# A gated linear recurrence and a top-1 expert layer: chunk scores by one product per head, rows sorted by expert as they come, fixed places per expert

## The chip, the core and the metric

The kernel runs on one core of a Trainium2 chip. A core has TensorE (PE in the profile; its weight loads stand apart as PEld), VectorE (DVE), ScalarE (ACT), GpSimd (POOL) and SyncE (SP), each with an instruction queue of its own that it works off in order, and DMA engines that move data between HBM and the on-chip memories. The metric is the device time of one execution in microseconds. All data are fp32.

## What is computed

Two parts. The first is a recurrence with a decay per key dimension, over 768 tokens, for 4 batches of 8 heads with 48 dimensions; the second sends each of the 3072 tokens (all heads side by side, 384 values) to the one of 8 experts with the largest cosine to its embedding.

```
f = 1.0 / (1.0 + np.exp(-f_logit))
for t in range(S):
    state = f[:, :, t, :, None] * state + np.einsum('bhd,bhe->bhde', k[:, :, t], v[:, :, t])
    y[:, :, t] = np.einsum('bhd,bhde->bhe', q[:, :, t], state)
...
logits = xn @ en.T / tau
expert_idx = np.argmax(logits, axis=1)
...
for e in range(E):
    mask = expert_idx == e
    h = np.maximum(x[mask] @ w1[e], 0.0)          # w1[e]: 384 x 1024
    out[mask] = gate_w[mask, None] * (h @ w2[e])  # w2[e]: 1024 x 384
```

## The kernel before

Attention works in chunks of 128 tokens. `attend` takes a group of two chunks of one batch with all 8 heads, and two batches run half a group apart, so that one's products fill the other's waits. f, k and q are loaded as they lie (tokens on the partitions) and turned by transposes on PE (`turn`). Inside a chunk the score of a pair s < t needs the product of f from s+1 to t. The kernel builds it in seven levels m = 1 to 64 (L199 to L229): at each level PE multiplies all of kp by half the columns of qp (L203, 8 products a level and group), DVE puts the pairs that belong to this level into the score tile `am` under a mask (L210), DVE and POOL multiply qp and kp by the decays of the next level (L220, L223, L225). So a level's products wait for the step before them. Then the state's increment (kp turned, L240, times v, L246), the output y from the state (L265, 48 rows) and the scores (L268, 128 rows) in turn, the row x stored to `x_rows` in HBM (L290), its squared length (L294) and its logits (L297 to L305).

Routing starts when all 24 chunks are through: the gate, each token's rank within its expert, and a product with one-hot matrices (L422 to L434) that turns positions into a list of source rows for 31 blocks of 128 places.

The experts: for each of 31 blocks, `hidden` reads the block's expert number into registers, loads w2 (w1 of all experts was loaded during attention), gathers 128 rows (L460), turns them (L470) and multiplies them by w1 (L477, the rows stationary, 512 columns moving); `result` turns h (L492), multiplies it by w2 (L498) and scatters the rows to `out` (L507). Block j+1's `hidden` is issued ahead of block j's `result`.

The order on each engine is that of the program, as far as the scheduler of the tile layer leaves it; a tile's buffers are handed on in turn, and the one who wants one back waits for its last reader.

## Time and profile before

| | us |
|---|---|
| three timed runs | 1111.2, 1114.74 (median), 1120.58 |
| the profiled execution, first to last instruction | 1119.0 |
| attention | 9.4 to 630 |
| routing | 630 to 678 |
| experts | 678 to 1119 |

The rows are those of the profiled execution; times in it are microseconds from its first instruction. A group of rows names the line, the engine, the operation, what is written and read with shapes, and what the engine waited for ahead of it. [...]

### The profile page before, as it was taken

Reading aid. Unit: us, or ns where it says so; the run is one execution under the profiler, and the core shown is the slowest. Engines: PE = TensorE matmul, PEld = TensorE weight load, DVE = VectorE, ACT = ScalarE, POOL = GpSimd, SP = SyncE. Lnnn points to the kernel's source line nnn. Section 1 sums busy time; section 2 is a strip of 40 time slices with the busy share of each in tenths; the row PEclk is TensorE's granted clock in tenths of the full one; section 3 lists DMA queues with packets and bytes.
Section 4 is the critical chain, followed back from the end, with each engine's and each line's share of the span. In section 5 each row is a group of like instructions: output and inputs, shape, how many; then the busy total and the mean of one; then the engine's idle time right before and its main releaser. Section 6 shows DMA issues by size and latency. Waiting matters only on the chain. (4 is left out here: it accounts for less than half of the span.)

```text
span 1119.0 us, 10918 instructions
## 1 busy us (share of the span) xinstructions
PE 901.7 (81%) x4218; PEld 675.3 (60%) x4218; DVE 417.8 (37%) x523; ACT 125.2 (11%) x236; POOL 287.2 (26%) x315
## 2 busy tenths in 40 slices
PE   4687889888797978879897647888888888888886
PEld 3576878777686877768776543444444444444443
DVE  7558464563727385463723341111111111111111
ACT  3001101010101101010100100111111111111110
POOL 6325424151505245151511011111111111111101
PEclk8788787776858687775865558999999999999999
DMA  9907303030303123010100005444444444444430
GB/s 221 258 23 218 64 8 71 1 71 1 71 1 71 40 32 71 1 29 1 29 15 1 15 16 189 141 141 140 141 141 141 135 141 136 139 141 141 141 115 0
DMA packets 140802, 96.47 MB, mean 86 GB/s; under 512 B 102120, under 2 KB 134095, under 8 KB 140752
## 3 DMA queue, kind: packets, MB, share of 16 engines
q1 hardware_dynamic: 135280, 80.22, 27.3%
q0 software_dynamic: 5312, 15.54, 3.7%
q8 instruction: 34, 0.56, 0.2%
q14 instruction: 16, 0.13, 0.0%
q10 hardware_dynamic: 160, 0.01, 0.0%
HBM read 86.32 MB, written 10.81 MB: 87 GB/s over the span
## 5 line engine op out<-in xcount | busy, mean ns | idle before, releaser
L203 PE MATMUL sc<-qz,kp 128*128 128x128 f32 x1344 | 235.7, 347 | 82.1 <-DVE qz L220 68.0
L203 PEld LDWEIGHTS sc<-qz,kp 128*128 128x128 f32 x1344 | 222.0, 256 | 91.6 <-POOL kp L223 42.9
L498 PE MATMUL y_ps<-w_sb,hT 128*128 128x384 f32 x496 | 167.2, 491 | 39.5 <-issue 38.2
L477 PE MATMUL h_ps<-w_sb,xT 128*128 x372 | 169.6, 606 | 18.8 <-DVE xT L472 18.8
L210 DVE COPY_PREDICATED a<-mask,sc 128x1024 f32<-128x1024 uint8 x84 | 135.6, 1614 | 111.7 <-PE sc L203 110.6
L498 PEld LDWEIGHTS y_ps<-w_sb,hT 128*128 128x128 f32 x496 | 91.8, 190 | 103.5 <-issue 44.0
L223 POOL TENSOR_TENSOR kp<-kp,dec 128x512 f32<-128x512 f32 x72 | 85.6, 1189 | 180.8 <-PE sc L203 172.0
L477 PEld LDWEIGHTS h_ps<-w_sb,xT 128*128 128x128 f32 x372 | 69.0, 192 | 101.9 <-issue 75.8
L220 DVE TENSOR_TENSOR qz<-qz,dec 64x512 f32<-64x512 f32 x144 | 120.0, 833 | 2.2
L460 POOL DMA_INDIRECT xin<-x_rows,src_row x31 | 31.6, 1020 | 332.5 <-PE x_ps L470 315.9
L494 DVE COPY hT<-ht_ps 128x1024 f32<-128x1024 f32 x31 | 38.0, 1224 | 198.1 <-PE ht_ps L492 198.1
L268 PE MATMUL y<-v_ld,a 128*128 128x48 f32 x384 | 105.0, 379 | 0.0
L265 PE MATMUL y<-state,qz 48*128 48x48 f32 x320 | 96.8, 397 | 0.0
L268 PEld LDWEIGHTS y<-v_ld,a 128*128 128x128 f32 x384 | 80.4, 268 | 13.3
L472 DVE COPY xT<-x_ps 128x384 f32<-128x384 f32 x31 | 17.3, 558 | 179.5 <-PE x_ps L470 179.4
L265 PEld LDWEIGHTS y<-state,qz 48*128 48x128 f32 x320 | 72.3, 280 | 13.8 <-issue 0.9
L286 DVE TENSOR_TENSOR av<-y,av 128x768 f32<-128x768 f32 x12 | 11.5, 958 | 131.3 <-PE y L268 131.3
L485 ACT ACTIVATE h<-h_ps 128x1024 f32<-128x1024 f32 x31 | 31.8, 1025 | 218.2 <-PE h_ps L477 218.2
L507 POOL DMA_INDIRECT out_dram<-y,dst_row x31 | 31.3, 1011 | 63.2 <-ACT y L506 55.3
L506 ACT ACTIVATE y<-y_ps,gpos 128x384 f32<-128x384 f32 x31 | 18.0, 581 | 202.8 <-PE y_ps L498 195.9
L294 ACT ACTIVATE sq<-av 128x384 f32<-128x384 f32 x24 | 12.4, 516 | 242.6 <-DVE av L286 242.6
L492 PEld LDWEIGHTS ht_ps<-ident,h 128*128 128x128 f32 x248 | 29.0, 141 | 16.3 <-issue 15.8
(133 smaller groups left out, 616.8 us busy)
## 6 DMA issues: line engine op xcount, KB each, us to landing
w_sb<-in_moe_w_dram SPq DMA_DIRECT2D x39, 1536.0 KB, 7.9
f_ld<-in_f_logit_dram SPq DMA_DIRECT2D x24, 192.0 KB, 4.4
k_ld<-in_k_dram SPq DMA_DIRECT2D x24, 192.0 KB, 3.9
q_ld<-in_q_dram SPq DMA_DIRECT2D x24, 192.0 KB, 4.5
v_ld<-in_v_dram SPq DMA_DIRECT2D x24, 192.0 KB, 3.3
x_rows<-av POOLq DMA_DIRECT2D x12, 384.0 KB, 3.4
xin<-x_rows,src_row POOLq DMA_INDIRECT x31, 6.5
out_dram<-y,dst_row POOLq DMA_INDIRECT x31, 5.8
```

The source lines that it names most:

```text
L203: nc.tensor.matmul(sc[:, n].rearrange("p r (b i) -> p (r b) i", i=m), lhsT=kp[:, n * P : n * P + P], rhs=qp[:, n].rearrange("p r (b z i) - ...
L210: nc.vector.copy_predicated(am.rearrange("p n r (b z i) -> p (n r) b z i", z=2, i=m)[:, :, :, 1], masks[lv].rearrange("p (b i) -> p b i", ...
L220: nc.vector.tensor_tensor(qv[r, :, par], qv[r, :, par], dv[r, :, :, 0:1].to_broadcast(shp), ALU.mult)
L223: nc.gpsimd.tensor_tensor(kv, kv, dv[:, :, :, 1:2].to_broadcast([P, NT, nb, m]), ALU.mult)
L265: nc.tensor.matmul(o, lhsT=qp[r, n, par], rhs=state[r, hp], start=True, stop=False)
L268: nc.tensor.matmul(o, lhsT=am[:, n, par], rhs=v_ld[:, c, 2 * hp + par], start=first, stop=True)
L460: nc.gpsimd.indirect_dma_start(out=xin, out_offset=None, in_=x_rows[:], in_offset=bass.IndirectOffsetOnAxis(ap=src_row[:, j : j + 1], axis=0),
L477: nc.tensor.matmul(h_ps[:, fh * 512 : fh * 512 + 512], lhsT=xT[:, c * P : c * P + P], rhs=w1f[:, ds(ek * (DC * F) + (c * F + fh * 512), 512)],
L485: nc.scalar.activation(h, h_ps, AF.Relu)
L494: nc.vector.tensor_copy(hT, ht_ps)
L498: nc.tensor.matmul(y_ps[:, 0:D], lhsT=hT[:, c * P : c * P + P], rhs=w2_sb[:, c], start=(c == 0), stop=(c == FC - 1),)
L507: nc.gpsimd.indirect_dma_start(out=out[:], out_offset=bass.IndirectOffsetOnAxis(ap=dst_row[:, j : j + 1], axis=0), in_=y, in_offset=None, ...
```

## The change

The old kernel body becomes `general_path`, which runs at the end if a flag is set. In front of it stands a new body.

Attention goes one chunk of one batch (a step, 24 in all, the four batches in turn) at a time. `decays` turns f, takes its sigmoid and makes two scans along the tokens on DVE: `suf`, the product of f from a token to the chunk's end, and `at`, the product from the start divided by that of the whole chunk. With k times the first (kz, on POOL) and q times the second (qa, on DVE), one product per head gives all scores of a chunk (`scores`); two heads lie on partitions 0 to 63 and 64 to 127, and a causal mask is multiplied in on the way from PSUM. The state of two heads is kept as a block-diagonal tile, so that one product of 96 columns serves two heads (`update2`, `outputs`). The steps of several chunks are issued interleaved, one stage apart.

Each expert has 448 places in `x_sorted` in HBM, filled with zeros early on. After every four steps `route` and `place` find the positions of 512 tokens, and POOL scatters their rows there. After the last, the gate values and token numbers are scattered to `meta`, one transfer per step, and read back as `gmeta` and `gtok`. The experts then run one after the other over 448 places: `hidden` has w1 stationary and 448 columns of x moving, so that h comes out turned already, and `result` has h stationary (112 places) and w2 moving. The flag is set if an expert has over 448 tokens or a chunk's decay product is at most 1e-15.

```diff
 @with_exitstack
-def tile_hgrn2_outer__then__cosine_router_kernel(
+def general_path(
     ctx: ExitStack,
     tc: tile.TileContext,
...
+    CAP = 448
+    NB = 4
+    PB = CAP // NB
+    NOROW = 1.0e6
+    PC_MIN = 1.0e-15
...
+    x_sorted = nc.dram_tensor("x_sorted", (E * CAP, D), FP32, kind="Internal").ap()
+    meta = nc.dram_tensor("meta", (E * CAP, 2), FP32, kind="Internal").ap()
...
+            def decays(i):
...
+                L = live[i]
+                ft = f_sb[i % NF]
+                body = ft[:, 0 : HP * W].rearrange("p (n w) -> p n w", w=W)
+                nc.scalar.activation(body[:, :, 1:W], turn(lds["f"][i % NLD]), AF.Sigmoid)
+                suf = work.tile([P, HP * W + 1], FP32, name="suf", bufs=3)
+                nc.vector.tensor_tensor_scan(
+                    suf[:, ::-1], ft[:, ::-1], revone[:, ::-1], 0.0, ALU.mult, ALU.add
+                )
+                pc = pc_all[:, i]
...
+                nc.vector.reciprocal(d1.rearrange("p (n w) -> p n w", w=W)[:, :, 0], pc)
+                at = work.tile([P, HP * W], FP32, name="at", bufs=2)
+                nc.vector.tensor_tensor_scan(at, ft[:, 0 : HP * W], d1, 0.0, ALU.mult, ALU.add)
+                pcm = work.tile([P, HP, 2], FP32, name="pcm", bufs=3)
...
+            def keys(i):
+                L = live[i]
+                kps = turn(lds["k"][i % NLD])
+                kz = work.tile([P, HP, P], FP32, name="kz", bufs=3)
+                kraw = work.tile([P, HP, P], FP32, name="kraw", bufs=2)
+                nc.scalar.copy(kraw, kps)
+                z = L["suf"][:, 1 : HP * W + 1].rearrange("p (n w) -> p n w", w=W)[:, :, 1:W]
+                nc.gpsimd.tensor_tensor(kz, kraw, z, ALU.mult)
+                qps = turn(lds["q"][i % NLD])
+                qa = work.tile([P, HP, P], FP32, name="qa", bufs=3)
+                a = L["at"].rearrange("p (n w) -> p n w", w=W)[:, :, 1:W]
+                nc.vector.tensor_tensor(qa, qps, a, ALU.mult)
+                L["kz"], L["qa"] = kz, qa
...
+            def scores(i):
+                L = live[i]
+                kz, qa = L["kz"], L["qa"]
+                sc = [ps_s.tile([P, HP, P], FP32, name=f"sc{par}") for par in range(2)]
+                for hp in range(HP):
+                    for par in range(2):
+                        r = slice(64 * par, 64 * par + 64)
+                        nc.tensor.matmul(sc[par][:, hp], lhsT=kz[r, hp], rhs=qa[r, hp], start=True, stop=True)
+                am = work.tile([P, 2, HP, P], FP32, name="am", bufs=2)
+                for par in range(2):
+                    nc.vector.tensor_tensor(
+                        am[:, par], sc[par], causal.unsqueeze(1).to_broadcast([P, HP, P]), ALU.mult
...
+            def update2(i):
...
+                add = ps_s.tile([P, HP, 2, DH], FP32, name="add")
+                for hp in range(HP):
+                    nc.tensor.matmul(
+                        add[:, hp], lhsT=L["kt"][:, hp], rhs=L["v"][:, 2 * hp : 2 * hp + 2], start=True, stop=True
+                    )
...
+            def outputs(i):
+                b, c = steps[i]
+                L = live[i]
+                y = ps_s.tile([P, HP, 2, DH], FP32, name="f_y")
+                if c:
+                    for hp in range(HP):
+                        nc.tensor.matmul(
+                            y[:, hp], lhsT=L["qa"][:, hp], rhs=L["st"][:, hp],
+                            start=hp == 0, stop=False, skip_group_check=True,
+                        )
+                for hp in range(HP):
+                    for par in range(2):
+                        nc.tensor.matmul(
+                            y[:, hp, par], lhsT=L["am"][:, par, hp], rhs=L["v"][:, 2 * hp + par],
+                            start=c == 0 and hp == 0 and par == 0, stop=True, skip_group_check=True,
+                        )
+                x = work.tile([P, D], FP32, name="f_x", bufs=10)
+                nc.scalar.copy(x, y.rearrange("p n r d -> p (n r d)"))
+                sq = work.tile([P, D], FP32, name="f_sq")
+                nc.scalar.activation(sq, x, AF.Square, accum_out=ssq[:, i : i + 1])
+                L["x"] = x
+            lgs = {}
...
+            def place(g):
+                sl = slice(g * B, g * B + B)
+                shp = [P, B, E]
+                rank = lgs[g][:, 1]
+                nc.tensor.matmul(rank, lhsT=tri, rhs=hot[:, sl], start=True, stop=False)
...
+                    nc.gpsimd.indirect_dma_start(
+                        out=x_views[s][:],
+                        out_offset=bass.IndirectOffsetOnAxis(ap=pos_i[:, s : s + 1], axis=0),
+                        in_=live[s]["x"],
+                        in_offset=None,
+                        bounds_check=E * CAP - 1,
+                        oob_is_err=False,
+                    )
...
+            for i in range(-2, NST + 3):
+                at(i + 3, lambda j: load(j) if j >= 3 else None)
+                if i == 0:
+                    nc.sync.dma_start(
+                        out=x_sorted.rearrange("(j p) d -> p j d", p=PB),
+                        in_=zero.unsqueeze(1).to_broadcast([PB, E * NB, D]),
+                    )
+                    nc.sync.dma_start(
+                        out=meta.rearrange("(p j) t -> p j t", p=P), in_=norow
+                    )
+                if i in (8, 14):
+                    weights((i - 8) // 6)
+                at(i + 2, decays)
+                at(i, update)
+                at(i + 1, keys)
+                at(i + 1, carry)
+                at(i, scores)
+                at(i - 2, logits)
+                at(i - 1, outputs)
+                at(i, update2)
+                at(i - 2, logits2)
+                if i - 2 >= 0 and (i - 2) % B == B - 1:
+                    route((i - 2) // B)
+                    place((i - 2) // B)
...
+            for s in range(NST):
+                nc.gpsimd.indirect_dma_start(
+                    out=meta_views[s][:],
+                    out_offset=bass.IndirectOffsetOnAxis(ap=pos_i[:, s : s + 1], axis=0),
+                    in_=mrow[:, s],
+                    in_offset=None,
+                    bounds_check=E * CAP - 1,
+                    oob_is_err=False,
+                )
+            nc.scalar.dma_start(out=gmeta, in_=meta.rearrange("(e p j) t -> p e j t", e=E, p=PB))
+            nc.vector.tensor_copy(gtok, gmeta[:, :, :, 0])
...
+            nc.vector.tensor_tensor(bad[:, NST * HP :], cnt[:, 0, 0], lim, ALU.is_gt)
+            nc.vector.tensor_scalar(
+                bad[:, 0 : NST * HP], pc_all.rearrange("p s n -> p (s n)"), PC_MIN, None, ALU.is_le
...
+            nc.tensor.matmul(cnt[:, 1, 0, 0:1], lhsT=ones, rhs=badp, start=True, stop=True)
+            nc.vector.tensor_scalar(flag, cnt[0:1, 1, 0, 0:1], 1.0, None, ALU.min)
...
+            def columns(e):
+                xTs[e] = mp.tile([P, DC, CAP], FP32, name="xTs")
+                for c in range(DC):
+                    ps = ps_x.tile([P, CAP], FP32, name="x_tp")
+                    for j in range(NB):
+                        nc.tensor.transpose(
+                            ps[:, j * PB : j * PB + PB], xs[e][:, j, c * P : c * P + P], ident[0:PB, 0:PB]
+                        )
+                    nc.vector.tensor_copy(xTs[e][:, c], ps)
...
+            def hidden(e):
+                w1 = wts[e][0]
+                hTs[e] = mp.tile([P, FC, CAP], FP32, name="hTs")
+                for f in range(FC):
+                    ps = ps_h.tile([P, CAP], FP32, name="h_ps")
+                    for c in range(DC):
+                        nc.tensor.matmul(
+                            ps, lhsT=w1[:, c, f * P : f * P + P], rhs=xTs[e][:, c], start=c == 0, stop=c == DC - 1
+                        )
+                    if f % 2:
+                        nc.vector.tensor_scalar(hTs[e][:, f], ps, 0.0, None, ALU.max)
+                    else:
+                        nc.scalar.activation(hTs[e][:, f], ps, AF.Relu)
...
+            def result(e):
+                w2 = wts[e][1]
+                for j in range(NB):
+                    ps = ps_y.tile([PB, D], FP32, name="y_ps")
+                    for f in range(FC):
+                        nc.tensor.matmul(
+                            ps, lhsT=hTs[e][:, f, j * PB : j * PB + PB], rhs=w2[:, f], start=f == 0, stop=f == FC - 1
+                        )
+                    y = mp.tile([PB, D], FP32, name="f_yo", bufs=6)
...
+                        out=out_views[e * NB + j][:],
+                        out_offset=bass.IndirectOffsetOnAxis(ap=gtok[:, e, j : j + 1], axis=0),
+                        in_=y,
+                        in_offset=None,
+                        bounds_check=N - 1,
+                        oob_is_err=False,
+                    )
...
+            rows(0)
+            rows(1)
+            columns(0)
+            for e in range(E):
+                hidden(e)
+                if e + 1 < E:
+                    columns(e + 1)
+                if e + 2 < E:
+                    rows(e + 2)
+                    weights(e + 2)
+                result(e)
+    redo = nc.values_load(flag[0:1, 0:1], min_val=0, max_val=1, skip_runtime_bounds_check_because="a minimum with one")
+    with tc.If(redo):
+        general_path(tc, q, k, v, f_logit, moe_expert_emb, moe_tau, moe_w1, moe_w2, out)
```

What it does to the order. First PE in attention. Before, one group's seven levels stand against another's, with y products of the two operands in turn (kp and qz are k and q with their decays, sc the scores of a level, ps transposes and the increment):

```order
L135 MATMUL ps_590<-ident_58,q_ld0_80 128x128 x4
L203 MATMUL sc_603<-qz1_89,kp_308 128x128 x8
L203 MATMUL sc_618<-qz0_88,kp_558 128x128 x8
L203 MATMUL sc_633<-qz1_89,kp_308 128x128 x8
L203 MATMUL sc_648<-qz0_88,kp_558 128x128 x8
L240 MATMUL ps_664<-ident_58,kp_308 128x128 x4
L246 MATMUL ps_663<-v_ld_298,kt_669 64x48 x8
L240 MATMUL ps_679<-ident_58,kp_308 128x128 x4
L246 MATMUL ps_663<-v_ld_298,kt_684 64x48 x8
L203 MATMUL sc_694<-qz0_88,kp_558 128x128 x8
```

Now, one whole step (tp are transposes; f_x the rows of the step two back, am the masked scores of the step before; the score rows, eight in all, alternate):

```order
L648 MATMUL tp_1560<-f_ident_65,f_f0_108 128x128 x4
L726 MATMUL tp_1574<-f_ident_65,kz_1461 128x128 x4
L648 MATMUL tp_1581<-f_ident_65,f_k3_107 128x128 x4
L648 MATMUL tp_1590<-f_ident_65,f_q3_103 128x128 x4
L711 MATMUL sc0_1599<-qa_1470,kz_1461 128x128
L711 MATMUL sc1_1600<-qa_1470,kz_1461 128x128
...
L776 MATMUL tp_1612<-f_ident_65,f_x_1506 128x128 x3
L754 MATMUL f_y_1618<-st_1382,qa_1380 128x96 x4
L760 MATMUL f_y_1618<-f_v_1159,am_1484 128x48 x8
L738 MATMUL add_1635<-f_v_1250,f_kt_1579 128x96 x4
L787 MATMUL lg_1642<-f_enT_70,f_xT_1616 128x8 x3
```

The level products and the alternation are gone; the operands of every product were made a step earlier. Then ACT from routing to the experts. Before:

```order
L299 COPY xT<-ps 128x384
L79 ACT_TABLE_LOAD
L79 ACTIVATE rn<-ssq 128x24
L305 COPY logit<-ps 128x8
L365 ACT_TABLE_LOAD
L365 ACTIVATE logit<-logit 128x192
L485 ACTIVATE h<-h_ps 128x1024 x2
L506 ACTIVATE y<-y_ps,gpos 128x384
```

Now:

```order
L778 COPY f_xT<-tp 128x384
L608 ACT_TABLE_LOAD
L608 ACTIVATE f_rn<-f_ssq 128x24
L923 ACT_TABLE_LOAD
L923 ACTIVATE f_logit_sb<-f_logit_sb 128x192
L984 ACTIVATE hTs<-h_ps 128x448
L936 DMA gmeta<-meta 112x8x8
L984 ACTIVATE hTs<-h_ps 128x448 x3
L995 ACTIVATE f_yo<-y_ps,gmeta 112x384 x4
```

The load of `gmeta` stands between the first Relu of expert 0 and its next three. What it waits for stands at the end of POOL's attention work, where before there were a product of the one-hot matrices and the first gathers:

```order
masks.py:65 MEMSET tri 128x128
L340 IOTA io_i 128x128
masks.py:66 AFFINE_SELECT tri<-tri 128x128
L344 IOTA tok_i 128x24
L290 DMA x_rows<-av 128x2x384
L426 TENSOR_TENSOR vals<-blk_hot,gate 128x24x31
L460 DMA xin<-x_rows,src_row 128x384 x6
L507 DMA out_dram<-y,dst_row 3072x384
```

and now:

```order
L697 TENSOR_TENSOR kz<-kraw,suf 128x512
L805 TENSOR_TENSOR f_cum<-f_cum,hot 128x8 x4
L820 DMA x_sorted<-f_x,f_pos_i 3584x384 x4
L928 DMA meta<-mrow,f_pos_i 3584x2 x24
L996 DMA out_dram<-f_yo,gtok 3072x384 x32
L1017 TENSOR_LOAD flag
L1018 COMPARE_AND_BRANCH
```

24 scatters to `meta` follow the last row scatters, and the output's scatters follow those.

## Rows read from the trace of the kernel before

**Rows 1.** Table of stages; after the colon the stretch's length.

```profile
core 0: us, PE busy (x) PEld busy (x) DVE busy (x) ACT busy (x) POOL busy (x), PEclk, DMA share, GB/s
9.40:630.00 620.60, 510.24 (x2938) 457.63 (x2937) 336.53 (x372) 65.89 (x159) 216.92 (x241) 0.73 0.26 56
630.00:678.00 48.00, 17.57 (x76) 16.25 (x76) 19.92 (x72) 4.91 (x10) 5.74 (x5) 0.50 0.21 71
678.00:1119.00 441.00, 373.54 (x1204) 201.07 (x1203) 54.69 (x61) 49.78 (x62) 59.40 (x59) 0.99 0.39 129
```

**Rows 2.** Groups by line: operands, count; busy us, mean ns; idle before, releaser.

```profile
L203 PE MATMUL sc<-qz,kp 128*128 128x128 f32 x1344 | 235.7, 347 | 82.1 <-DVE qz L220 68.0 <-POOL dec L225 6.4 <-DVE qz L180 3.8
L210 DVE COPY_PREDICATED a<-mask,sc 128x1024 f32<-128x1024 uint8 x84 | 135.6, 1614 | 111.7 <-PE sc L203 110.6
L223 POOL TENSOR_TENSOR kp<-kp,dec 128x512 f32<-128x512 f32 x72 | 85.6, 1189 | 180.8 <-PE sc L203 172.0 <-DMA x_rows<-av 8.8
```

**Rows 3.** Timeline, PE, experts, one block: start us, length us, records, [idle before].

```profile
713.16 5.42 PE L477 MATMUL h_ps<-w_sb,xT 128*128 x12 [0.65 <-DVE xT L472]
718.41 1.04 PE L492 MATMUL ht_ps<-ident,h 128*128 128x128 f32 x8
720.81 5.40 PE L498 MATMUL y_ps<-w_sb,hT 128*128 128x384 f32 x16 [1.36 <-issue]
726.05 0.49 PE L470 MATMUL x_ps<-ident,xin 128*128 128x128 f32 x3
727.19 5.42 PE L477 MATMUL h_ps<-w_sb,xT 128*128 x12 [0.65 <-DVE xT L472]
```

**Rows 4.** Timeline, PE, attention, at the full level of the clock.

```profile
300.93 2.02 PE L203 MATMUL sc<-qz,kp 128*128 128x128 f32 x16 [2.70 <-DVE qz L220]
345.14 1.04 PE L135 MATMUL ps<-ident,k_ld 128*128 128x128 f32 x8
371.63 1.88 PE L268 MATMUL y<-v_ld,a 128*128 128x48 f32 x16
373.44 0.42 PE L265 MATMUL y<-state,qz 48*128 48x48 f32 x2
373.79 0.42 PE L268 MATMUL y<-v_ld,a 128*128 128x48 f32 x2
```

**Rows 5.** Timeline, PE, at the half level: the first steps and routing.

```profile
9.43 1.97 PE L135 MATMUL ps<-ident,f_ld 128*128 128x128 f32 x8
18.31 3.83 PE L203 MATMUL sc<-qz,kp 128*128 128x128 f32 x16 [3.82 <-DVE qz L180]
656.74 10.47 PE L432 MATMUL inv_ps<-vals,row_hot 128*128 128x62 f32 x48 [10.95 <-DVE row_hot L427]
```

**Rows 6.** Groups by line and shape, DVE: a plain product from PSUM.

```profile
L180 DVE TENSOR_TENSOR qz<-ps,ft 64x512 f32<-64x512 f32 x48 | 33.0, 688 | 1.2
```

**Rows 7.** Timeline, POOL, the first three gathers.

```profile
669.09 1.10 POOL L460 DMA_INDIRECT xin<-x_rows,src_row  x1 [15.71 <-issue]
670.50 1.03 POOL L460 DMA_INDIRECT xin<-x_rows,src_row  x1 [0.30 <-issue]
671.83 0.99 POOL L460 DMA_INDIRECT xin<-x_rows,src_row  x1 [0.30 <-issue]
```

**Rows 8.** Two stretches of attention, columns as in rows 1.

```profile
316.80:330.40 13.60, 13.60 (x48) 11.48 (x47) 1.46 (x3) 0.00 (x0) 0.21 (x1) 0.50 0.00 0
344.10:357.70 13.60, 9.19 (x75) 8.29 (x74) 12.12 (x11) 1.07 (x2) 8.76 (x11) 1.00 0.49 74
```

**Rows 9.** The page's 40 equal slices: GB/s moved.

```profile
GB/s 221 258 23 218 64 8 71 1 71 1 71 1 71 40 32 71 1 29 1 29 15 1 15 16 189 141 141 140 141 141 141 135 141 136 139 141 141 141 115 0
```

**Rows 10.** The page's DMA issues: KB each, median us from issue to landing.

```profile
x_rows<-av POOLq DMA_DIRECT2D x12, 384.0 KB, 3.4
xin<-x_rows,src_row POOLq DMA_INDIRECT x31, 6.5
```

**Rows 11.** Timeline, PE, the last two blocks.

```profile
1099.56 10.59 PE L498 MATMUL y_ps<-w_sb,hT 128*128 128x384 f32 x32
```

**Rows 12.** Timeline, PE, the transposes after the first.

```profile
11.23 1.93 PE L135 MATMUL ps<-ident,k_ld 128*128 128x128 f32 x8
13.02 0.66 PE L135 MATMUL ps<-ident,q_ld 128*128 128x128 f32 x4
```

263 lines of the change are left out of this document (262 added, 1 removed).

## The prediction

> **What bounds the kernel now.** I read the table of stages first, then the groups by line, then TensorE's timeline in one stretch of each stage. The table splits the span of 1119.0 us [rows 1]: 621 us of attention in which PE is busy for 510 us, 48 us of routing in which PE has 18 us of work, and 441 us of experts in which PE is busy for 374 us. In attention the largest group is the level products of L203, 84 levels of 8 products, 235.7 us [rows 2]; each level waits for the DVE and POOL steps of the one before, and the DVE group L210 exists for them alone. So attention is a PE stage with waits, at a mean granted clock of 0.73 [rows 1]. The experts are a plain PE stage: a block is 12 records of 512 columns in 5.25 us, 8 transposes, then 16 records of 384 columns in 5.24 us, and the next block's first product starts 14.03 us after this one's [rows 3]; 31 blocks make 435 us.
>
> An fp32 product is two records, a transpose one. [...]
>
> **The change part by part.**
>
> *Attention.* The seven levels go: no L203, L210, L220, L223; and no y products that alternate between 48-row and 128-row operands at 0.35 us a product [rows 4]. Instead each of 24 steps (one chunk of one batch, all heads) has on PE: 12 transposes of f, k, q and 3 of x, 4 more of kz in 20 of the steps, 8 score products, 8 am products of 48 columns, 3 logit products, and in 20 steps each 4 products of 96 columns for the state's part of y and for the update. The 96-column ones have no row; between 0.117 us (48) and 0.126 us (128) a record I take 0.97 us for four. Three logit products have as many weight loads as six records, so 0.76 us. Over all steps at the full level: 440 transposes 57.2, scores 24 x 2.02 = 48.5, am 24 x 1.88 = 45.1, 96 columns 40 x 0.97 = 38.8, logits 24 x 0.76 = 18.2, ranks 24 records 2.9: 211 us. At the half level the same counts give 108 + 92 + 84 + 72 (0.226 a record) + 31 + 5 = 392 us.
>
> Is PE the bound there? A step is about 9 us of PE. DVE has two scans of 517 elements, one product from PSUM and two masked ones, one add, and small ones. No row shows a scan: I bound it by 0.69 us (L180, a plain product) and 1.61 us (L210, twice the elements) [rows 2, 6], so DVE has 2 x 0.69 to 2 x 1.61, plus 3 x 0.69, plus about 1: 4.5 to 6.3 us. [...] POOL has kz at up to 1.19 us (L223) [rows 2], the state, three quarters of its elements, at 0.9, and in the mean one indirect scatter at 1.33 us [rows 7]: under 4 us. DMA: a step loads 0.79 MB, and the first slices moved 221 to 258 GB/s [rows 9]: 3.1 to 3.6 us. All hide under PE, a step ahead of it by the order of issue; if one of them took over 9 us, the stage would go at its pace.
>
> So the clock decides between 211 and 392. In the stage before, PE stayed at half through the alternating 48-column products (13.6 us busy of 13.6, granted 0.50), and held the full level where runs of 128-column products stood with waits between (9.2 us busy of 13.6, granted 1.00) [rows 8]. Of a new step, 16 transposes and the scores in one run are over 4 us of the second kind; the am and logit products, 2.6 us, are of the first. I take the middle of the means of the two stages, 0.73 and 0.99 [rows 1], rounded down to 0.85: 211 / 0.85 = 248 us. Ends: 211 (all full) and 289 (0.73).
>
> Around it: the first transpose stood at 9.4 us and the first product at 18.3 [rows 5]; the new chain (sigmoid, two scans, qa, scores) is about as long, and 28 transposes, 3.6 us, are done in it: net 15 us. The zero fill of x_sorted, 5.5 MB, is queued on SP behind load(3) and ahead of load(4): at 221 to 258 GB/s [rows 9] it takes 21 to 25 us from about 16 us, and decays(4) would want its f at 36 to 40: 0 to 10 us of waiting, I take 5. The last step drains through mask, y, x copy, transpose, copy, logits, then 13 small DVE operations of routing: 8 us. So the last positions exist at T0 = 15 + 248 + 5 + 8 = 276 us. Of the 48 us of routing the one-hot work is gone, but something takes its place.
>
> *From routing to the first expert.* POOL issues 4 row scatters at a pitch of 1.33 us, as the gathers before (1.41 from an idle start, then 1.33 us) [rows 7]; an indirect transfer lands some 6.5 us after its issue [rows 10], so rows(0) may start at T0 + 10.5; 0.69 MB take 3 us at the rate of the first slices and not under the 3.4 us of a transfer of half the size [rows 10], so about 5; transposes and copies 2: hidden(0) starts at T0 + 17.5. But behind the 4 scatters on POOL stand 24 meta scatters: 24 x 1.33 = 32 us, to T0 + 37, landed at T0 + 43. The load of gmeta is issued by ACT, in order, between the first and the second Relu of hidden(0), and waits for them all; the Relus of blocks 2, 4 and 6 are queued behind it, and on DVE the cast of gtok stands between blocks 1 and 3. With three PSUM buffers PE does blocks 0 to 4 (11.5 us, and some 3.5 more at the half level, to T0 + 32) and stands still until T0 + 44; the last three blocks come cold and behind gtok, 10 us: hidden(0) ends at T0 + 54, where 17.5 + 18.4 would have been 36. So 18 us of the routing come back here as a wait.
>
> *Experts.* 448 columns cost 448/512 of 437 ns, 383 ns a record: 48 records are 18.4 us; 64 records of 384 columns at 328 ns are 21.0 us [rows 3]; 12 transposes 1.5 us: 40.9 us an expert, 327 us for eight, against 435. The 8 h transposes of a block and its waits for hT and xT (1.36 and 0.65 us) go, because two experts' work alternates and three PSUM buffers stand behind each product; without that cover a block would pay such waits again, 8 x 2 us. Weights: 3.1 MB an expert in 41 us, 75 GB/s, where 141 flowed before [rows 9]; w2(e+2) waits for result(e) and then has 39 us. After hidden(0), 327 - 18.4 = 309 us are left.
>
> *End.* From the last product's end, 1110.15, to the span's end were 9 us [rows 11]; reading the flag and the branch over the old body I take as 1 us, between 0 and 5: the flag is there long before, and the chain ends with the last scatter.
>
> Sum: 276 + 54 + 309 + 10 = 649 us in the profiled execution. The median of the runs shown, 1114.74, is 4 us under the profiled span, so **645 us**.
>
> **The rivals.** (1) *Attention at the half clock*, 392 instead of 248: 793 us. Against it: the first 8 transposes of the kernel went at 0.246 us each, and after 8 more, with nothing else on PE but three 8-column ones, four took 0.66 us instead of 0.98 [rows 5, 12], so transposes raised the clock. [...] 10%. (2) *Score products in turn on rows 0-63 and 64-127 don't overlap their weight loads*, as the alternating y products did not: 0.35 us for 48 columns there against 0.235 in a plain run [rows 4]; for 128 columns, load and product one after the other, some 0.48 instead of 0.25 us, 192 times: +44 us, 693 us. Against it: those had rows in common, these have none. 12%. (3) *The old body runs as well*: the flag is set if an expert gets over 448 tokens or a decay product of a chunk is at most 1e-15. Then 649 + about 1110 = 1760 us, slower. It decides at the 449th token; on the reference's inputs I count 352 to 417 tokens an expert, and the least product is 6.6e-10. 2%. (4) *Cheaper*: full clock throughout and no wait at the fill: 649 - 37 - 5 = 607 us, or a little less if score products on the two halves run side by side. 11%. (5) *A wait in the step that I don't see* (POOL's scatters ahead of kz, loads behind the expert weights), 2 us a step: 697 us. 8%.
>
> **How the numbers follow.** The forecast, with its own ends of 610 and 690, has 57%; with rivals 2, 4 and 5 the range of 600 to 750 holds some 85%, and leaves out the half clock and the flag. The runs before lie within 0.8% of each other, so 1% is what can be told. Faster by over 1%: 97%; slower: 2%; same: 1%.
>
> **What would show it.** The table of stages: attention ends near 275 us at a granted clock of 0.8 to 0.9 with PE busy most of a step. Score products at 0.25 us each. The 24 meta scatters at 1.3 us on POOL, and PE idle for some 10 us in hidden(0), ended by ACT. Then a period of 41 us an expert. No instruction of the old body in the trace. The forecast is wrong if a step takes over 12 us with PE waiting, or if the period of the experts is not 41 us.

## The result, and the profile after

The changed kernel takes **609.29 us** (median of four runs, 607.39 to 611.12) where the kernel before takes 1112.97 us (1098.44 to 1120.58): a ratio of 0.550, 95% interval 0.546 to 0.554. Forecast were 645 us in a range of 600 to 750, and faster. The profiled execution has a span of 605.5 us at a mean granted clock of 0.913. The granted clock is PEclk of the profile, the share of TensorE's full clock; the full level is 1.00 in it, the half level 0.50.

The table of stages of the changed kernel; it answers to [rows 1], columns as there:

```profile
core 0: us, PE busy (x) PEld busy (x) DVE busy (x) ACT busy (x) POOL busy (x), PEclk, DMA share, GB/s
7.17:45.00 37.83, 28.18 (x194) 25.21 (x193) 23.50 (x39) 11.71 (x23) 7.70 (x10) 0.82 1.18 246
45.00:119.00 74.00, 70.31 (x582) 66.00 (x584) 49.77 (x85) 26.17 (x56) 33.52 (x40) 0.88 0.74 145
119.00:141.00 22.00, 22.00 (x216) 21.14 (x213) 18.02 (x28) 8.87 (x21) 9.22 (x10) 1.00 1.00 214
141.00:243.00 102.00, 91.25 (x711) 85.61 (x709) 54.13 (x109) 32.05 (x70) 40.44 (x53) 0.84 0.43 90
243.00:264.20 21.20, 3.70 (x17) 3.24 (x17) 3.75 (x14) 0.36 (x1) 15.66 (x16) 0.50 0.45 104
264.20:292.00 27.80, 23.09 (x52) 11.16 (x52) 2.60 (x6) 2.17 (x4) 11.73 (x12) 0.82 0.23 26
292.00:600.00 308.00, 299.82 (x932) 161.11 (x930) 29.91 (x50) 33.78 (x60) 30.16 (x32) 0.99 0.27 89
```

Attention now ends at 243 us instead of 630, still a PE stage: in 119:141 PE is busy without a gap and at the full level. Around that stretch the clock is at 0.82 to 0.88 and PE has gaps. Then 21 us pass with next to nothing on PE, the first expert's `hidden` takes 28, and the rest is PE work at 0.99, as the experts before.

TensorE's timeline of the changed kernel: a steady step, the end of a step with rank products, the first expert, the second:

```profile
start us, us, engine line op out<-in xcount [idle before <-releaser]
124.22 0.63 PE L648 MATMUL tp<-f_ident,f_f 128*128 128x128 f32 x4
126.12 1.16 PE L711 MATMUL sc<-qa,kz 64*128 64x128 f32 x16
127.22 0.55 PE L776 MATMUL tp<-f_ident,f_x 128*128 128x128 f32 x3
127.60 1.03 PE L754 MATMUL f_y<-st,qa 128*128 128x96 f32 x8
128.47 1.91 PE L760 MATMUL f_y<-f_v,am 128*128 128x48 f32 x16
130.21 1.10 PE L738 MATMUL add<-f_v,f_kt 128*128 128x96 f32 x8
131.15 0.76 PE L787 MATMUL lg<-f_enT,f_xT 128*128 128x8 f32 x6
131.76 0.63 PE L648 MATMUL tp<-f_ident,f_f 128*128 128x128 f32 x4
...
143.64 0.41 PE L811 MATMUL lg<-hot,f_tri 128*128 128x32 f32 x2 [1.49 <-DVE hot L803]
146.02 0.64 PE L812 MATMUL lg<-f_cum,f_ones 128*128 128x32 f32 x2 [1.55 <-POOL f_cum L805]
149.66 3.54 PE L760 MATMUL f_y<-f_v,am 128*128 128x48 f32 x16
...
261.62 2.76 PE L967 MATMUL x_tp<-f_ident,xs 112*128 112x112 f32 x12 [16.73 <-DMA xs<-x_sorted]
264.18 13.09 PE L978 MATMUL h_ps<-xTs,w 128*128 128x448 f32 x30
281.97 9.98 PE L978 MATMUL h_ps<-xTs,w 128*128 128x448 f32 x18 [4.71 <-ACT hTs L984]
...
313.64 18.20 PE L978 MATMUL h_ps<-xTs,w 128*128 128x448 f32 x48
331.68 0.93 PE L967 MATMUL x_tp<-f_ident,xs 112*128 112x112 f32 x8
353.53 2.79 PE L978 MATMUL h_ps<-xTs,w 128*128 128x448 f32 x7
```

Read start to start (a length also holds the end of the last record). A step takes 131.76 - 124.22 = 7.54 us. Its sixteen score records take 1.10 us, or 1.16 as a length, where sixteen had a length of 2.02 in the kernel before [rows 4]; 19 transposes 2.28 us (124.22 to 126.12 and 127.22 to 127.60), 0.12 each; am 1.74; an expert's period is 39.89 us. At 143.64 and 146.02 the two rank products of `place` stand among the score products and wait 1.5 us each, one for DVE's `hot`, one for POOL's `f_cum`; the am products behind them take twice their time. That step lasts from 139.31 to 155.97 us. The view that sums PE's waits in the changed kernel (us in total, times, longest):

```profile
PE x_tp L967 <- DMA xs<-x_sorted: 16.7, 1, 16.7
PE lg L811 <- DVE hot L803: 7.7, 5, 1.9
PE tp L881 <- DVE f_emb L878: 6.8, 1, 6.8
PE tp L648 <- DMA f_f<-in_f_logit_dram: 6.5, 3, 4.2
PE lg L812 <- POOL f_cum L805: 5.1, 5, 1.6
PE h_ps L978 <- ACT hTs L984: 4.7, 1, 4.7
```

The 6.8 us for `f_emb` are the start, ahead of PE's first instruction. So three kinds of waiting are left: the rank products (12.8 us, at six places), f behind the zero fill, and the change to the experts. At three of the six places both rank products wait some 1.5 us (71, 143 and 185 us), and PE is at the half level for 13 to 16 us behind them (0.50 to 0.53 in 74:87, 146:161.5 and 188.5:203). One wait of 1.88 us at 223.69 us is followed by the full level (1.00 in 223.5:240). The last product ends at 591.8; the span ends 13.7 us later. No instruction of the old body was run.

**Theory** before the experiments: attention came out shorter than forecast because score products on the two row halves run side by side; the rank waits and the half clock behind them, which the forecast lacked, ate part of that. **Rivals:** a 64-row product is cheap whatever stands beside it; the clock falls by itself and the waits cost only their 12.8 us.

### The profile page after: what moved, and what is told of

Same layout as the page of the kernel before. It is cut to its first block, busy times and chain, and to the rows that moved or that the text cites. A ratio compares the mean times of both kernels' runs of the same rounds, so it can differ in the third digit from the quotient of the medians.

```text
span 605.5 us, 6846 instructions
## 1 busy us (share of the span) xinstructions
PE 538.7 (89%) x2695; PEld 373.9 (62%) x2695; DVE 185.9 (31%) x356; ACT 118.5 (20%) x238; POOL 152.7 (25%) x192
## 4 chain that ended last, share of the span: by engine, by line
issue 47%; POOL 5%; POOLq 0%
POOL out_dram L996 5%; POOLq L996 0%; POOL meta L928 0%; POOLq L1017 0%
## 5 line engine op out<-in xcount | busy, mean ns | idle before, releaser
L991 PE MATMUL y_ps<-w,hTs 128*112 128x384 f32 x512 | 167.6, 486 | 0.0
L978 PE MATMUL h_ps<-xTs,w 128*128 128x448 f32 x384 | 150.5, 553 | 4.7 <-ACT hTs L984 4.7
L991 PEld LDWEIGHTS y_ps<-w,hTs 128*112 128x112 f32 x512 | 89.5, 177 | 70.5 <-issue 0.4
L978 PEld LDWEIGHTS h_ps<-xTs,w 128*128 128x128 f32 x384 | 74.9, 196 | 78.0 <-issue 70.6
L760 PE MATMUL f_y<-f_v,am 128*128 128x48 f32 x384 | 52.1, 294 | 0.6 <-ACT f_x L765 0.6
L760 PEld LDWEIGHTS f_y<-f_v,am 128*128 128x128 f32 x384 | 51.0, 214 | 0.9 <-ACT f_x L765 0.7
L658 DVE TENSOR_TENSOR_SCAN suf<-f_T,revone 128x517 f32<-128x517 f32 x24 | 31.0, 1296 | 36.9 <-ACT f_T L656 34.8
L668 DVE TENSOR_TENSOR_SCAN at<-f_T,fwd 128x516 f32<-128x516 f32 x24 | 40.4, 1688 | 0.5
L711 PE MATMUL sc<-qa,kz 64*128 64x128 f32 x384 | 36.4, 309 | 2.7 <-POOL kz L697 1.2
L714 DVE TENSOR_TENSOR am<-sc,causal 128x512 f32<-128x512 f32 x48 | 30.9, 672 | 5.3 <-PE sc L711 5.2
L820 POOL DMA_INDIRECT x_sorted<-f_x,f_pos_i x24 | 23.8, 993 | 20.1 <-DVE f_pos_i L818 14.6
L967 PE MATMUL x_tp<-f_ident,xs 112*128 112x112 f32 x96 | 13.5, 280 | 16.8 <-DMA xs<-x_sorted 16.7
```

Source lines behind the costliest of these rows:

```text
L658: nc.vector.tensor_tensor_scan(suf[:, ::-1], ft[:, ::-1], revone[:, ::-1], 0.0, ALU.mult, ALU.add)
L668: nc.vector.tensor_tensor_scan(at, ft[:, 0 : HP * W], d1, 0.0, ALU.mult, ALU.add)
L711: nc.tensor.matmul(sc[par][:, hp], lhsT=kz[r, hp], rhs=qa[r, hp], start=True, stop=True)
L714: nc.vector.tensor_tensor(am[:, par], sc[par], causal.unsqueeze(1).to_broadcast([P, HP, P]), ALU.mult)
L760: nc.tensor.matmul(y[:, hp, par], lhsT=L["am"][:, par, hp], rhs=L["v"][:, 2 * hp + par], start=c == 0 and hp == 0 and par == 0, stop=True, ...
L820: nc.gpsimd.indirect_dma_start(out=x_views[s][:], out_offset=bass.IndirectOffsetOnAxis(ap=pos_i[:, s : s + 1], axis=0), in_=live[s]["x"], ...
```

## The experiments

The runs were on three chips, on which the kernel before took 1105.4 us (the first four experiments), 1103.0 us (`after_again`, `e9`, `e10`, `e11`) and 1113.0 us (the last four). Ratios are to the kernel before beside each run; the changed kernel's own are 0.550 (above) and 0.5535 (`after_again`). Of `e13`, the fill in pieces on top of both edits, only the times are used.

**Score products in turn.**

```diff
-for hp in range(HP):
-    for par in range(2):
+for par in range(2):
+    for hp in range(HP):
         r = slice(64 * par, 64 * par + 64)
         nc.tensor.matmul(sc[par][:, hp], lhsT=kz[r, hp], rhs=qa[r, hp], ...)
```

> The eight score products of a step are issued in another order: the four of rows 0-63 first, then the four of rows 64-127; nothing else changes. Theory: in the changed kernel the two row halves run side by side because neighbours in the order use different rows; a group of 16 records starts 1.10 us before what follows it, where the plain price was 2.02. In turn they should go back to about 2.0 us, a steady step from 7.54 to about 8.4 us, and 24 steps add 15 to 24 us: 625 to 633 us. Rival: a 64-row product is cheap by itself, whatever its neighbour: the group stays near 1.1 us and the time at 609, within 3 us.

634.87 us (627.74 to 638.51), ratio 0.574 (0.570 to 0.578). Its PE timeline, at the full level:

```profile
138.97 1.71 PE L711 MATMUL sc<-qa,kz 64*128 64x128 f32 x16
140.61 0.55 PE L776 MATMUL tp<-f_ident,f_x 128*128 128x128 f32 x3
```

1.64 us for sixteen records instead of 1.10, and the group's busy time goes from 36.4 to 52.9 us: the order matters. In the changed kernel's trace the records of the two halves start in pairs, 6 to 7 ns apart, and a pair every 0.105 us (126.337 and 126.344, 126.449 and 126.455 us): neighbours on different halves overlap, and the rival falls as the whole explanation. But the price in turn is not that of the kernel before: by lengths (2.02 before, 1.71 in turn, 1.16 in alternation), of the 0.86 us that the changed kernel saves a step, 0.55 is the order; 0.31 remains, for products of 64 rows instead of 128 at the same columns, and is not explained here. The two halves also write two PSUM tiles (`sc0` and `sc1`), so that the edit changes the alternation of tiles as well, and no run separates the two. Against the tiles as the cause: the am products of the kernel before wrote two areas of PSUM by turns, too (L268, sixteen in 1.88 us [rows 4]), and were no faster than those of the changed kernel, which all write one tile (1.91 us). The other 7 to 9 us of the loss stand for the most part at the end of attention: PE is at the half level from 243.4 us to the last logits at 267.7 (0.51, busy for 23.7 of 24.3 us), where the changed kernel does the same work at the full level from 225.7 to 238.7, and `after_again` below, partly at the half level, in 17.8 us. The wait ahead of it was 0.52 us.

**Place later: half a step, then a step.**

```diff
 at(i, scores)
+if i - 3 >= 0 and (i - 3) % B == B - 1:
+    place((i - 3) // B)
...
     route((i - 2) // B)
-    place((i - 2) // B)
+place(NST // B - 1)
```

> place(g), with the two rank products, is issued one step later, behind that step's score products, so that POOL's cum and DVE's hot have a step's time. Theory: the ten waits of PE for hot (7.7 us) and f_cum (5.1 us) go, and with them the stretches at the half clock that follow them (in 45:119 and 141:243 the granted clock is 0.88 and 0.84; at 1.00 PE's 162 us there would be some 20 us shorter): attention ends 20 to 33 us earlier, 576 to 590 us in all. Rival A: the clock falls for another reason, and only the waits go: 594 to 599 us. Rival B: the wait is handed on (DVE's queue between scans, the rank tile's only buffer): 603 to 610 us.

618.76 us (616.58 to 619.3), ratio 0.560 (0.557 to 0.563): none of the three. The rank products now stand behind the scores and wait all the same, here in that run's PE timeline:

```profile
68.94 1.16 PE L711 MATMUL sc<-qa,kz 64*128 64x128 f32 x16
71.36 0.41 PE L811 MATMUL lg<-hot,f_tri 128*128 128x32 f32 x2 [1.25 <-DVE hot L803]
73.73 0.64 PE L812 MATMUL lg<-f_cum,f_ones 128*128 128x32 f32 x2 [1.97 <-POOL f_cum L805]
```

In all 13.4 us, ten times: PE passes from the last logits to the end of the scores in 3 us, DVE does its six small operations for `hot` around a scan (three ahead of it and three behind, the last at 70.55 us), and POOL's four sums come after that (72.00 to 73.95). The edit also had a flaw: the loop already reaches the last group, so that the added line issues its place twice, four row scatters more; the first rows came 6.5 us later (a wait of 18.9 us against 12.4 in `after_again`), which is most of what the run lost.

The second try puts `place(g)` behind the next step's logits, with room for all groups in the tile of logits and ranks (and the same flaw at the end):

```diff
+lgall = ps_s.tile([P, NST // B + 1, 2, B, E], FP32, name="lg")
-    lgs[g] = ps_s.tile([P, 2, B, E], FP32, name="lg")
+    lgs[g] = lgall[:, g]
...
     route((i - 2) // B)
-    place((i - 2) // B)
+if i - 3 >= 0 and (i - 3) % B == B - 1:
+    place((i - 3) // B)
```

> The changed kernel once more, unaltered, as the yardstick for the runs beside it: the first four experiments ran on another chip than its first timing, where the kernel before took 1105 us instead of 1113, and in one of them the time of single runs lay 12 us apart. Theory: 605 to 613 us, with runs within 1% of each other. Rival: its time depends on where the half-clock stretches fall, and it varies by over 1% from chip to chip or run to run, as the one with the fill in pieces did (605 to 617); then differences of under 10 us in the first four runs say nothing.

> place(g) behind the logits of the next step, a whole step of 7.5 us after route(g), with room for all groups' logits and ranks in one PSUM tile, so that the next group's logits do not wait for the rank to be read; x has 12 buffers instead of 10. Place one half step later left the ten waits as they were (13.4 us for 12.8), as hot and f_cum come 4 and 6 us after the logits. Theory: now both are there, the ten waits go, and the clock stays at the full level through 45:243, since each half-clock stretch there begins within 2 us behind such a wait: attention ends near 210 to 220 us instead of 243 and the kernel takes 572 to 590 us. Rival A: the clock falls all the same and only the waits go: 594 to 598. Rival B: the four scatters on POOL now stand ahead of another kz and PE waits for that: 605 to 610.

The changed kernel again: 610.97 us (607.11 to 611.47), ratio 0.5535 (0.551 to 0.556), so the yardstick holds within 1%. Place a step later: **578.95 us** (578.1 to 582.12), ratio 0.526 (0.523 to 0.529), 32 us less. Its table of stages, over what were the stretches with waits:

```profile
45.00:119.00 74.00, 72.04 (x668) 67.76 (x669) 55.02 (x97) 29.12 (x63) 38.92 (x46) 0.98 0.88 171
119.00:205.00 86.00, 85.40 (x824) 81.74 (x822) 61.46 (x110) 33.45 (x76) 44.40 (x54) 1.00 0.66 140
```

and that of `after_again` over the same:

```profile
45.00:119.00 74.00, 69.13 (x568) 65.09 (x569) 47.67 (x84) 24.76 (x54) 33.82 (x39) 0.88 0.73 141
119.00:205.00 86.00, 79.92 (x633) 75.33 (x632) 53.25 (x90) 27.42 (x60) 37.84 (x45) 0.84 0.73 151
```

824 records against 633 in the same 86 us, PE busy for 85.4 of them, granted 1.00 instead of 0.84. The last logits begin at 206.2 us instead of 244.0. Of these 38 us the rank waits ahead of that point were 11.1; the other 27 are PE's busy time, which falls from 214.6 us (granted 0.85) to 187.1 (0.95) for the same products: the half clock behind the waits is gone with them. Rivals A and B fall. The kernel keeps 32 of the 38 us, since PE now waits 20.0 us for the first rows instead of 12.4 (in part from the place issued twice, see the runs with both edits).

**The load of gmeta off ACT.**

```diff
-nc.scalar.dma_start(out=gmeta, in_=meta...)
-nc.vector.tensor_copy(gtok, gmeta[:, :, :, 0])
...
 rows(1)
+nc.sync.dma_start(out=gmeta, in_=meta...)
 columns(0)
...
     columns(e + 1)
+if e == 0:
+    nc.vector.tensor_copy(gtok, gmeta[:, :, :, 0])
```

> The load of gmeta is issued by SP behind rows(1) instead of by ACT, and the cast to gtok stands behind columns(1) on DVE, so that no Relu of the first expert is queued behind the 24 meta scatters. Theory: PE's wait of 4.7 us in hidden(0) goes, and the records behind it run at the full clock: hidden(0) takes about 20 us instead of 27.6, the time falls by 5 to 9 us to 600 to 604. Rival: the wait moves to the first evictions of result(0), which need gmeta (landing about 284 us): PE goes on into three PSUM buffers, some 16 us of work, so nothing should be lost; if it is, the time stays within 2 us of 609.

611.41 us (609.72 to 612.03), ratio 0.554 (0.551 to 0.557): no change. The scheduler of the tile layer put the cast ahead of two of DVE's Relus, and PE waited 10.5 us for DVE instead. DVE's timeline of that run:

```profile
269.76 0.62 DVE L980 TENSOR_SCALAR hTs<-h_ps 128x448 f32<-128x448 f32 x1 [4.81 <-PE h_ps L976]
288.53 0.18 DVE L1012 CAST gtok<-gmeta 112x32 int32<-112x32 f32 x1 [18.14 <-DMA gmeta<-meta]
288.62 1.15 DVE L980 TENSOR_SCALAR hTs<-h_ps 128x448 f32<-128x448 f32 x2
```

So the cast went to POOL, whose scatters are the only readers of gtok:

```diff
-nc.vector.tensor_copy(gtok, gmeta[:, :, :, 0])
+nc.gpsimd.tensor_copy(gtok, gmeta[:, :, :, 0])
```

> The load of gmeta by SP behind rows(1), and the cast to gtok by POOL, which alone needs it, so that neither the Relus of ACT nor those of DVE in hidden(0) can stand behind the 24 meta scatters. With the cast left on DVE the scheduler had put it ahead of two Relus, and PE waited 10.5 us for DVE in place of 4.7 us for ACT. Theory: the wait goes; hidden(0) runs through in 18.4 us plus what the first records at the half clock cost: about 21 us instead of 27.6 in the first trace, 5 to 9 us less than the unaltered kernel beside it. Rival: the first evictions of result(0) need gmeta 20 us after hidden(0) began; if three PSUM buffers (16 us of work) do not reach, part of the wait comes back there and the gain is under 3 us.

**598.56 us** (597.13 to 599.53), ratio 0.543 (0.541 to 0.546), 12.4 us less than `after_again`. Its PE timeline:

```profile
264.33 19.22 PE L976 MATMUL h_ps<-xTs,w 128*128 128x448 f32 x48
283.39 0.93 PE L965 MATMUL x_tp<-f_ident,xs 112*128 112x112 f32 x8
```

The first `hidden` runs through in 19.1 us, where `after_again` needed 30.9 (265.13 to 296.02, with a wait of 9.8 us). The gain is above what I expected, as the wait there was 9.8 us and not the 4.7 of the first trace: in the first the rows came 4.3 us later (16.7 us of waiting for xs against 12.4), and what ends the wait in `hidden` in both is the last of 24 meta scatters.

**Both edits, and the last place once.**

> Both edits at once, place a whole step later and gmeta by SP with the cast on POOL. Theory: the two waits have nothing in common, and the gains add up: 565 to 583 us. Rival: the clock decides; if the first expert starts cold behind 20 us of scatters and loads whatever is done, the second edit gives nothing and the time equals that of place a step later alone, within 2 us.

> The two edits of the run with both, but the last group's place is issued once; there, as in the two runs with place later, it stood twice, so that four row scatters of 1.3 us and two rank products came double at the end of attention, and PE waited 19 to 20 us for the first rows instead of 12.4. Theory: 5 to 7 us of that wait go: 563 to 567 us, 40 to 46 us less than the unaltered kernel (611 on that chip). Rival: the rows' load is late for another reason (the expert weights or the meta scatters on the same DMA engines): 569 to 572 us.

Both: **571.34 us** (570.55 to 572.58), ratio 0.519 (0.517 to 0.521); 39.6 us less than `after_again`, 4.8 short of the sum of the two gains. With the doubled place out (the added line at the loop's end taken away): 569.15 us (564.17 to 575.75), ratio 0.514 (0.509 to 0.519), not told apart from the run before. The four scatters and the two products are gone, and from the last logits to the first transposes of x it is 22.6 us instead of 26.5. That is 3.9 of the 5 to 7 us that the theory asked, and the time lies in the rival's range: PE still waited 17.2 us for the rows, where `after_again` waited 12.4. The loads were issued 6.5 us after the last scatter's end, in `after_again` 2.2 us after it, and in the first trace of the changed kernel 5.8 us; what makes these 4 us come and go stays open.

**The fill in pieces.**

```diff
-if i == 0:
+if 0 <= i < 4:
+    o = i * E * CAP // 4
     nc.sync.dma_start(
-        out=x_sorted.rearrange("(j p) d -> p j d", p=PB),
-        in_=zero.unsqueeze(1).to_broadcast([PB, E * NB, D]))
+        out=x_sorted[o : o + E * CAP // 4].rearrange("(j p) d -> p j d", p=PB),
+        in_=zero.unsqueeze(1).to_broadcast([PB, E, D]))
+if i == 3:
     nc.sync.dma_start(out=meta.rearrange(...), in_=norow)
```

> The zero fill of x_sorted, 5.5 MB in one transfer, becomes four of 1.4 MB, one a step, ahead of the loads of steps 3 to 6; the meta fill goes with the last. Theory: the load of f for step 4 no longer waits behind the whole fill; PE's wait of 4.2 us at 38.8 us goes and the half clock around it: 4 to 9 us less, 600 to 605 us. Rival: the 16 DMA engines are full in the first 45 us (246 GB/s) whatever the order, so the wait is spread over several steps and the time stays within 2 us of 609.

> As the run with both edits and one last place, and the zero fill in four pieces, one a step. In the unaltered order the fill in pieces gave 605 to 617 us, no verdict. Theory: where no other wait is left, the waits for f (3.8 us in all) and the half clock from 26.7 to 43.8 us behind the fill go: 4 to 10 us less than without the pieces. Rival: in the first 45 us the DMA engines are the limit, and the pieces only move the wait to later steps (in the first try PE's waits for f fell by 4 us, but others of 3 us came): within 2 us of the run without them, or up to 4 us slower.

In the changed kernel 616.41 us (605.27 to 617.39), not told apart from it; on top of both edits 584.26 us (579.57 to 590.26), ratio 0.527 (0.523 to 0.532), slower than without the pieces by more than both intervals. PE's waits for f did fall, from 6.6 us in `after_again` to 2.4, and in the first 45 us PE did 33.5 us of work instead of 29.4. But the scheduler laid the steps behind it out in another order, in which each waits for its own `kz`, for ACT's `f_T` and for its own `am`. The PE timeline of the first of these runs:

```profile
58.29 1.16 PE L711 MATMUL sc<-qa,kz 64*128 64x128 f32 x16 [0.47 <-POOL kz L697]
64.48 0.66 PE L648 MATMUL tp<-f_ident,f_q 128*128 128x128 f32 x4 [0.37 <-ACT f_T L656]
67.44 1.16 PE L711 MATMUL sc<-qa,kz 64*128 64x128 f32 x16 [0.47 <-POOL kz L697]
```

A step there takes 67.44 - 58.29 = 9.15 us instead of 7.54. Three steps there (40.18 to 67.44 us) lose 4.6 us so, about what the waits for f gave back. So the runs do not tell what the fill alone costs. That the order is also what makes the run on top of both edits 15 us slower is not shown.

**512 places.** `CAP = 512` in the place of 448.

> 512 places per expert instead of 448, nothing else changed: the part of the forecast on the experts by itself. By the prices of before a record of w1 goes from 383 to 437 ns, 384 of them: +20.7 us; the 64 records of an expert with w2 moving stay at 328 ns, only with 128 rows stationary instead of 112; transposes +0.8 us; the fill has 6.3 MB instead of 5.5, 3 us more in the first 45 us, perhaps seen. Theory: 20 to 26 us more than the unaltered kernel, 629 to 637 us. Rival: moving columns are not the limit, but weight loads are (177 to 196 ns each, in their shadow): under 10 us more.

640.19 us (639.41 to 640.84), ratio 0.579 (0.574 to 0.584): 29 us more, above the 20 to 26 expected. Of its PE and POOL timelines:

```profile
328.16 20.76 PE L978 MATMUL h_ps<-xTs,w 128*128 128x512 f32 x48
348.76 1.04 PE L967 MATMUL x_tp<-f_ident,xs 128*128 128x128 f32 x8
...
266.58 0.98 POOL L928 DMA_INDIRECT meta<-mrow,f_pos_i  x1 [2.70 <-DMA meta<-mrow,f_pos_i]
272.65 0.98 POOL L928 DMA_INDIRECT meta<-mrow,f_pos_i  x1 [5.09 <-DMA meta<-mrow,f_pos_i]
```

48 records take 20.60 us instead of 18.04, 20.5 us over eight experts: the expected term, 20.7, holds, and the rival falls. The rest is at the change to the experts: POOL's meta scatters were held up for 8 us by earlier ones, and PE's wait for ACT in the first `hidden` was 14.5 us against 9.8.

**No branch.** The reading of the flag, the branch and the old body are left out, so that inputs over 448 tokens an expert are not served.

```diff
-redo = nc.values_load(flag[0:1, 0:1], min_val=0, max_val=1, ...)
-with tc.If(redo):
-    general_path(...)
```

> The branch on the flag and the old body behind it are left out; the flag is still computed. The rare inputs that need the old body are not served by this kernel. From the last product's end to the span's end the changed kernel has 13.7 us, the kernel before 9 us, and I had priced the branch at 1 us, between 0 and 5. Theory: the 4.7 us between these two are the branch and what the engines do around it: 603 to 607 us where the unaltered kernel has 607 to 611, the tail 9 us. Rival: they belong to the last scatter and the closing of the program, and the time stays within 1 us; or the code of the old body costs something early (fetching of instructions), then over 5 us go.

604.48 us (602.38 to 607.11), ratio 0.546 (0.541 to 0.552); the intervals overlap with the changed kernel's. The profiles tell it apart: in this run and in `after_again` ACT's last copy starts at the same 596.13 us, and the spans end at 605.3 and 609.7. The branch, with the reading of the flag and the old body behind it, costs 4.4 us, all behind the last scatter.

## Why the prediction came out as it did

The time lay 6% under the forecast and inside the range; the mechanism (a PE stage without the levels, routing given back in part as a wait in the first expert, experts at the price of their columns) was right, and sizes were off. By its steps:

- **Attention's PE work** was the largest miss: "211 us at the full level". At the prices of the steady step it is 440 transposes x 0.12 = 52.8, 24 x 1.10 = 26.4, 24 x 1.74 = 41.8, 20 x 0.87 + 20 x 0.94 = 36.2, 24 x 0.61 = 14.6, ranks 2.9: 175 us. Of the 36 us, 22 are the scores, priced from a row with 128-row operands [rows 4]. The fourth rival had named this ("or a little less if score products on the two halves run side by side"); the first experiment puts a good half of the difference (0.55 of 0.86 us a step) down to the order. That this rival's 607 us is nearly the time is luck: it stood on the full clock throughout and no wait at the fill, and neither came. The second rival, that the halves don't overlap, is refuted by the pairs of records: a score product takes 0.14 us in alternation, not 0.48. The price of each kind of product was a length in [rows 4] at the full level and in [rows 5] at the half level, where no row had 48 columns: sixteen records at L432's 0.218 us made 3.49 us. The runs showed 3.34 us for sixteen am records at the half level (149.66 to 153.00 us) and 0.21 for a transpose (from 155.97 us), not 0.246.
- **The clock**, 0.85 taken: PE was busy 210.5 us from 7.17 to 240 for these 175, so 0.83 in effect (granted mean 0.87). The size came out right by luck, as the reason was wrong: I mixed two stages' means by kinds of products, but steps of these same products, without waits, ran at the full level (1.00 in 119:141; in `e9` 0.98 in 45:119 and 1.00 in 119:205). The half level began behind waits. Which waits it follows is not settled: one of 1.88 us was followed by the full level in the changed kernel and by the half level in `after_again` (0.51 in 226.2:236.6), and in the first experiment the half level came behind one of 0.52 us and stayed for nearly 24 us of work without gaps. So steps without waits held the full level where they had it, and did not always regain it at once. The first rival fell: with 19 of the step's 46 PE operations transposes, the stage held the full level (1.00 in 119:141). My argument against it, that transposes raised the clock, is not shown: in the kernel before the granted clock reads 1.00 from the first transpose on (9.43:13.00), while they took 0.246 us each; why they were slow there stays open.
- **The wait at the fill**, 5 us taken: 6.5 us for f in three places. **Start and drain**, 15 + 8 us: 13.6 us (243.4 - 210.5 less the waits for f and for ranks).
- **Not in the sum:** the rank products. I counted them as 2.9 us of work, and not that `place` stands directly behind `route` and that PE is there before DVE and POOL. Ten waits, 12.8 us, and with the clock behind them 32 us or more. That was my fifth rival in kind (a wait in the step), not in place. The sign that I had given for being wrong, a step of over 12 us with PE waiting, did appear at the rank products, in three steps of 16 to 17 us each. The other work of DVE and POOL hid under PE as forecast: 6.2 and 3.2 us a step by the busy time in 119:141, though the second scan, 1.79 us, lies above its bound of 1.61. Positions existed at 243.4 us instead of 276: too much work in the sum and waits left out of it partly cancelled.
- **From routing to the first expert**, T0 + 54: T0 + 48.4. `hidden(0)` began at T0 + 20.8 instead of 17.5; the 24 meta scatters had their pitch of 1.28 us; PE stood still from T0 + 34 to T0 + 38.6, where T0 + 32 to T0 + 44 was forecast. The step that failed is the landing: ACT issued the load 1.7 us after the last scatter's end, not 6 us after. The last blocks took the 10 us forecast. That the queue of ACT and DVE is the cause is shown by the run with the cast on POOL.
- **Experts**, 309 us: 300.0. The period is 39.89 us against 40.9 (records 0.376 and 0.323 us, 12 transposes 1.2 us): some 7.5 us, and the first expert's transposes I had counted twice.
- **End**, 10 us: 13.7. The branch was priced 1 us, between 0 and 5, an estimate without a row; with the flag's reading and the old body it is 4.4.

In sum -32.6, -5.6, -9.0, +3.7: from 649 to 605.5 us.

## What to carry to other kernels

Before pricing an in-order engine's step, look for the one small operation in it whose operand comes last from a neighbour: here two products of 0.33 us held the engine for 1.5 us each, and the time lost behind them at the half clock was larger than the wait (27 us against 11.1 up to the last logits). A load that waits for a long list of transfers belongs on a queue with nothing urgent behind it, and what reads it on the engine that alone needs it (the run with the cast on POOL took 12.4 us less); writing it later in the program is not enough where a scheduler sets the order. After an edit that should only move a transfer, compare the order of the steps too, since that may cost as much as the transfer gains: with the fill in pieces three steps lost 4.6 us, the waits for f gave back 4.2.

## What the runs showed of the chip

- Products on rows 0-63 and rows 64-127 issued in alternation take 0.073 us a record of 128 columns, in turn 0.107; with 128-row operands it was 0.126 [rows 4] (each the length of a group of sixteen, divided by sixteen).
- The scans of 517 and 516 elements took 1.30 and 1.69 us in the mean (1.23 and 1.79 in a steady step); the bound from the nearest rows had been 0.69 to 1.61 each.
- POOL's indirect scatters are issued 1.28 us apart, whether a row has 8 bytes (meta) or 1536 (x); but in the run with 512 places two of them waited 2.7 and 5.1 us for earlier ones; that the longer loads of rows then in flight are the reason is not shown.
- A branch that is not taken, with the reading of its flag and the old body behind it, lengthened the end by 4.4 us, though its flag was known at 245 us, some 350 us before.
